# Twenty-six more filler matmuls on TensorE: twelve behind the first scores of the attention, fourteen ahead of the first gathered rows

## The chip, the cores and the metric

The kernel runs on one core of one Trainium2 chip. The metric is the time of one execution on the device in microseconds (us), the median of three runs. Smaller is better.

## What is computed

Three layers follow each other: an attention whose queries are pooled in pairs, a mixture of eight experts with one expert for each token, and a dense feed-forward layer.

```python
q_pool = q.reshape(B, H, S // 2, 2, D).mean(axis=3)        # B, H, S, D = 2, 8, 1152, 64
scores = np.matmul(q_pool, k.transpose(0, 1, 3, 2)) / np.sqrt(D)
attn = softmax(scores)                                     # max subtracted, sum + 1e-9
x = np.matmul(attn, v)                                     # brought to 1152 tokens x 512
...
do_compute = x @ w_skip > 0                                # the other tokens pass unchanged
e_idx = np.argmax(xc @ w_gate, axis=1)                     # one of 8 experts
y = gate_w * (np.maximum(xc @ w1[e], 0) @ w2[e])           # w1 512 x 1024, w2 1024 x 512
out[do_compute] = xc + y
...
h = x @ w_in                                               # 512 x 2048
return (h * np.tanh(softplus(h))) @ w_out                  # 2048 x 512
```

## The kernel before

**Order.** The program fixes the order of every engine's work by the order in which the Python code issues it. An engine takes its instructions one after the other, and a semaphore holds an instruction back until what it reads is there. TensorE is PE in the profile, VectorE is DVE, ScalarE is ACT, GpSimd is POOL, and SP is the queue that issues most DMAs.

**Attention** (lines 55 to 470). The work is cut into 72 tiles, nine for each of the eight heads. A tile is 128 pooled queries against all 1152 keys. The loop of line 405 runs once for each tile n, and in one round TensorE gets, in this order: the transposes of tile n-3 (`turn`, line 175, from the fourth round on), some matmuls with the values (`av_step`, line 216, once whole heads are ready), and the scores of tile n (`scores`, line 145). The scores of a tile fill the PSUM tile `s`, of which there is one; DVE scales them, writes them to SBUF as `scp` and takes their minimum (line 148, called the eviction below), and only then may the scores of the next tile be written. ACT then takes the exponential (line 159), and copies the transposed tile out of PSUM (line 198). Before the first scores, ten filler matmuls run (line 400); the loads of the first head arrive meanwhile.

**Filler matmuls.** `keep_warm` (line 473) issues n matmuls of a 128x128 tile of ones by a 128x512 tile of zeros, both bf16. Nobody reads what they write: in the attention the target is the tile `tp`, which the first transposes overwrite later, and in the routing a tile `warm`. `WARM` (line 43) holds the counts for the four places.

**Routing** (lines 478 to 621). Behind the last projection of the attention, DVE works out for each token its expert and its place in that expert's list. Matmuls on TensorE count and order the tokens (lines 511, 515, 537). Fillers stand before, between and behind these: 9 at line 509, 5 at line 532 and 15 at line 542. Then the first lists of tokens are known, and POOL issues two gathers of rows (line 625, `first(idx)`), which read the rows that the attention has just written to DRAM. TensorE next transposes the first gathered rows (line 1304, `turn(ps)`), does a column of the ordering (line 587), and then the first matmul of the first expert (line 637, `up`, tile `sa`), for which ACT copies the transposed rows (line 1305). Behind it stands the large part of the ordering (line 587 again). It gives the remaining lists: POOL then gathers the other rows, and behind its first further gather stand the memsets (line 830) for which SP waits with the loads of the experts' remaining weights (line 831).

**Experts and feed-forward layer** (lines 814 to 920, 1013 to 1215). The experts' matmuls lie in branches that are taken according to how many tokens an expert has. The feed-forward layer is a loop of 48 steps with matmuls of line 1101 and line 1155.

Of the kernel before, what the change touches and what calls it, by code (L numbers as in the profile page):

```python
# [39 lines left out]
BF16 = mybir.dt.bfloat16  # L40
KEEP = (0, 1, 4, 5, 2, 3, 6, 7)
PASS = ((0, 0), (0, 1), (1, 0))
WARM = (10, 9, 5, 15)
SPARE = (1.45, 1.45, 1.9, 1.45, 1.45, 0.75, 0.0, 1.75, 1.45)
OFF = (4, 7, 10, 13, 16, 19, 22, 25)
EARLY = (13, 16, 19, 45, 30, 39, 48, 57, 62, 65, 68)
# [8 lines left out]
def attention(tc, io, lg, rows, wdec, zero_out, late, xr, yg):  # L55
    nc = tc.nc
    with ExitStack() as ctx:
# [13 lines left out]
        tp = ps_t.tile([P, 2, 512], F32, name="tp")  # L71
# [3 lines left out]
        def load_wb(h):  # L75
            st["wb", h] = one.tile([P, XW], F32, name="wb", tag="wb", bufs=2)
            nc.sync.dma_start(st["wb", h], io["wb"][h])
# [5 lines left out]
        def load(h):  # L83
            for b, r in enumerate((xr, yg)):
                st["qr", h, b] = r.rearrange("p t f -> p (t f)")[:, :S].rearrange("p (a c) -> p a c", a=2)
                nc.sync.dma_start(st["qr", h, b], io["qt"][h, b])
            for b in range(B):
                st["k", h, b] = kq.tile([P, Q], F32, name=f"ks{b}", tag=f"ks{b}")
                nc.sync.dma_start(st["k", h, b], io["kt"][h, b])

        def load_v(h):
            vt = raw.tile([P, B, KC, D], F32, name="vt", tag="vt", bufs=2)
            nc.sync.dma_start(vt, io["vt"][h])
            st["v", h] = vt
# [15 lines left out]
        def first_head():  # L110
            near = (slice(0, Q // 2), slice(0, 320))
            far = tuple(slice(c.stop, Q) for c in near)
            ld = nc.sync.dma_start
            qr = []
            for b, r in enumerate((xr, yg)):
                qr.append(r.rearrange("p t f -> p (t f)")[:, :S].rearrange("p (a c) -> p a c", a=2))
                st["qr", 0, b] = qr[b]
                st["k", 0, b] = kq.tile([P, Q], F32, name=f"ks{b}", tag=f"ks{b}")
            ld(qr[0][:, :, near[0]], io["qt"][0, 0, :, :, near[0]])
            for c in (slice(0, HQ), slice(HQ, Q)):  # L120
                ld(st["k", 0, 0][:, c], io["kt"][0, 0, :, c])
            ld(qr[1][:, :, near[1]], io["qt"][0, 1, :, :, near[1]])
            ld(st["k", 0, 1], io["kt"][0, 1])
            for b in range(B):
                ld(qr[b][:, :, far[b]], io["qt"][0, b, :, :, far[b]])
            q_sum(0, 0, near[0], nc.vector)
            q_sum(0, 1, near[1], nc.gpsimd)
            for b in range(B):
                q_sum(0, b, far[b], nc.gpsimd)

        def scores(h, t):
            if t == 4:
                ops = [(slice(0, D), st["q", h, 0][:, 4 * P :], 0), (slice(D, P), st["q", h, 1][:, :D], 1)]
            else:
                b, c = t // 5, P * t if t < 4 else P * (t - 5) + D
                ops = [(slice(0, P), st["q", h, b][:, c : c + P], b)]
            scp = sc.tile([P, S], F32, name="scp", tag="scp")
            mx = sm.tile([P, 1], F32, name="mx", tag="mx")
            st["x", h, t] = scp, mx
            for j in range(2):  # L140
                cs = slice(HQ * j, HQ * j + HQ)
                for o, w, b in ops:
                    for half in range(2):
                        r = slice(D * half, D * half + D)
                        st["tick"] = nc.tensor.matmul(  # L145
                            s[o, half, j, :HQ], w[r], st["k", h, b][r, cs], start=True, stop=True
                        ).ins
            nc.vector.tensor_scalar(  # L148
                scp.rearrange("p (a c) -> p a c", a=4),
                s.rearrange("p a j c -> p (a j) c")[:, :, :HQ],  # L150
                -EXP_SCALE, -NEG, op0=ALU.mult, op1=ALU.min, accum_out=mx,
            )
# [16 lines left out]
        def turn(h, t, eight, nine, opened=None):  # L169
            e = st.pop(("e", h, t))  # L170
            for i in range(KC):
                for a in range(2):
                    q = slice(D * a, D * a + D)
                    to = eight[a][:, D * i : D * i + D] if i < 8 else nine[a]
                    nc.tensor.matmul(  # L175
                        to, e[q, P * i : P * i + P], io["ident"][q, q], start=i < 8 or a != opened, stop=True,
                        is_transpose=True, skip_group_check=True,
                    )
# [11 lines left out]
        def put_e(h, t, ks, v):  # L190
            b, tt = t // 5, t % 5
            if t == 4:
                for g in range(2):
                    to = etile(h, g)[:, ks, :, 256:].rearrange("p k b c -> p b k c")
                    nc.scalar.copy(to, v[:, :, :, 32 * g : 32 * g + 32])
            else:
                to = etile(h, tt // 2)[:, ks, b, P * (tt % 2) : P * (tt % 2) + P]
                nc.scalar.copy(to.rearrange("p k (a c) -> p a k c", a=2), v)  # L198
# [85 lines left out]
        def finish(h):  # L284
            norm(h)
            project(h, ovs, range(4), 1)
            xt = scale(h, ovs, 0)
            put(h, xt, 0, 9)
            dec_ops.insert(0, (0.28, lambda: logits(h, xt)))
# [109 lines left out]
        nseq = len(seq)  # L399
        keep_warm(nc, io, tp[:, 0], WARM[0])  # L400
        first_head()
# [3 lines left out]
        for n in range(nseq + 1):  # L405
            pos = n % 9
            h = n // 9
            m = n - 3
            run = n < nseq
            trn = 0 <= m < nseq  # L410
            if run:
                nxt = h + 1 < H
                if pos == 0 and nxt:
                    load(h + 1)
                if pos == 1:
                    load_wb(h)
                if pos == 4 and nxt:
                    sums = [0, 1]
                if pos == 7 and nxt:
                    load_v(h + 1)  # L420
            c = slice(512 - D, 512)
            if trn:
                opened = None
                if avq and avq[0][3] and not pend:
                    opened = avq[0][1]
                    c = slice(c.start - spot * D, c.stop - spot * D)
                    spot += 1
                else:
                    spot = 0
                turn(*seq[m], tph, [x[:, c] for x in ov], opened)  # L430
                put_e(*seq[m], slice(0, 8), tpk)
            if pend:
                finish(pend.pop(0))
            else:
                av_step((3 if len(avq) >= 9 else 2) if run else 6)
            if 0 < n <= nseq:
                expo(*seq[n - 1])
            if trn:
                put_e(*seq[m], slice(8, KC), ovs[:, :, c].unsqueeze(2))
            if pos == 3:  # L440
                ext_copy()
            if trn:
                if m % 9 == 4:
                    av_start(seq[m][0], 0)
                if m % 9 == 8:
                    av_start(seq[m][0], 1)
            if run:
                scores(*seq[n])
                if n == 6:
                    dec_load(0)  # L450
                    dec_load(1)
                if n in EARLY:
                    zero_out(EARLY.index(n))
            st["used"] = False
            if run and not fin:
                dec_run(SPARE[pos])
            if run and not st["used"]:
                if sums and pos + len(sums) > 7:
                    beside(q_sum(h + 1, sums.pop(0), slice(0, Q), nc.gpsimd))
                elif side:  # L460
                    beside(side.pop(0)())
                elif sums:
                    beside(q_sum(h + 1, sums.pop(0), slice(0, Q), nc.gpsimd))
            if fin:
                hf = fin.pop(0)
                pend = [hf]
# [6 lines left out]
def keep_warm(nc, io, out, n):  # L473
    for _ in range(n):
        nc.tensor.matmul(out, io["ones"], io["blank"], start=True, stop=True)


def routing(tc, io, lg, rt, tmp, ps, first, second, turn, kept):
# [29 lines left out]
    W = (T + 1) * E  # L508
    keep_warm(nc, io, warm, WARM[1])
    for s in range(1, T + 1):  # L510
# [20 lines left out]
    )  # L531
    keep_warm(nc, io, warm, WARM[2])
    tk4 = tk.rearrange("p t (c j) -> p t c j", j=4)
# [7 lines left out]

    keep_warm(nc, io, warm, WARM[3])

# [854 lines left out]
```

## Time and profile before

| | us |
|---|---|
| median of three runs | 577.96 |
| the three runs | 577.7, 577.96, 579.11 |
| the profiled execution, its own time | 581.02 |
| span of the profiled execution, first to last instruction | 579.1 |
| TensorE busy in that span | 544.2 (94%) |
| mean granted TensorE clock in that span | 0.975 of full speed |

The granted clock is told as a share of 2.4 GHz: 1.00 is 2.4 GHz and 0.50 is 1.2 GHz. In a row of the timeline the first number is the start in us from the start of the span, the second how long it lasted, and xN how many instructions the row merges; a bracket at its end tells how long the engine was idle before and what ended that.

### The profile page before, as it was taken

Reading aid. Unit: us, or ns where it says so; the run is one execution under the profiler, and the core shown is the slowest. Engines: PE = TensorE matmul, PEld = TensorE weight load, DVE = VectorE, ACT = ScalarE, POOL = GpSimd, SP = SyncE. Lnnn points to the kernel's source line nnn. Section 1 sums busy time; section 2 is a strip of 40 time slices with the busy share of each in tenths; the row PEclk is TensorE's granted clock in tenths of the full one; section 3 lists DMA queues with packets and bytes.
Section 4 is the critical chain, followed back from the end, with each engine's and each line's share of the span. In section 5 each row is a group of like instructions: output and inputs, shape, how many; then the busy total and the mean of one; then the engine's idle time right before and its main releaser. Section 6 shows DMA issues by size and latency. Waiting matters only on the chain. (4 is left out here: it accounts for less than half of the span.)

```text
span 579.1 us, 12048 instructions
## 1 busy us (share of the span) xinstructions
PE 544.2 (94%) x4781; PEld 402.4 (69%) x4781; DVE 372.0 (64%) x709; ACT 358.1 (62%) x663; POOL 95.9 (17%) x98
## 2 busy tenths in 40 slices
PE   6799999999999999789969989999999999999994
PEld 3566666766676667336724655898899998999982
DVE  3488888888988886610010026699986677666663
ACT  3888888888888885110112012799877766666562
POOL 1213454334533311240000110000000000000000
PEclk8899999999999999989978999999999999999998
DMA  7568867997978771279976095455112200010001
GB/s 251 205 207 285 281 231 276 318 340 238 311 262 301 224 260 58 76 217 400 401 278 257 24 343 199 130 190 174 55 37 87 77 0 2 0 57 2 0 1 59
DMA packets 50358, 103.03 MB, mean 178 GB/s; under 512 B 14043, under 2 KB 15451, under 8 KB 50288
## 3 DMA queue, kind: packets, MB, share of 16 engines
q1 hardware_dynamic: 47760, 95.99, 48.3%
q0 software_dynamic: 1296, 3.75, 2.1%
q10 hardware_dynamic: 1232, 2.36, 1.2%
q8 instruction: 43, 0.70, 0.5%
q14 instruction: 27, 0.22, 0.1%
HBM read 85.49 MB, written 17.04 MB: 177 GB/s over the span
## 5 line engine op out<-in xcount | busy, mean ns | idle before, releaser
L148 DVE TENSOR_SCALAR_CACHE_REDUCE scp<-s 128x1152 f32<-128x1152 f32 x72 | 97.7, 1357 | 35.9 <-PE s L145 24.9
L1101 PE MATMUL ph<-xT,wi 128*128 128x384 f32 x576 | 108.5, 337 | 0.0
L1101 PEld LDWEIGHTS ph<-xT,wi 128*128 128x128 f32 x576 | 102.2, 188 | 4.2
L145 PE MATMUL s<-ks,qs 64*128 64x288 f32 (+1 forms) x640 | 90.9, 432 | 7.1 <-DVE scp L148 5.5
L159 ACT ACTIVATE scp<-scp,mx 128x1152 f32<-128x1152 f32 x72 | 90.5, 1257 | 8.1 <-DVE scp L148 7.9
L1155 PE MATMUL po<-wo,gh 128*128 128x512 f32 x288 | 90.3, 394 | 0.8 <-ACT gh L1140 0.7
L198 ACT COPY eT<-tp 128x1024 f32<-128x1024 f32 x63 | 63.8, 1013 | 29.5 <-PE tp L175 29.0
L145 PEld LDWEIGHTS s<-ks,qs 64*128 64x128 f32 (+1 forms) x640 | 49.1, 177 | 42.9 <-DVE scp L148 17.5
L216 PE MATMUL ov<-eT,vt 128*64 128x288 f32 x540 | 78.3, 417 | 0.0
L1155 PEld LDWEIGHTS po<-wo,gh 128*128 128x128 f32 x288 | 52.9, 188 | 10.3 <-ACT gh L1140 1.5
L175 PEld LDWEIGHTS tp<-cst,scp 64*128 64x128 f32 x1145 | 48.0, 141 | 13.6 <-issue 4.4
L1155 PE MATMUL po<-wo,gl 128*128 128x512 f32 x144 | 57.2, 397 | 0.0
L1125 ACT ACTIVATE u<-u 128x384 f32<-128x384 f32 (+1 forms) x49 | 25.4, 519 | 46.6 <-DVE u L1119 46.1
L1145 DVE TENSOR_TENSOR gl<-s,gh 128x384 fp32r<-128x384 f32 (+1 forms) x49 | 27.0, 550 | 41.7 <-ACT gh L1140 41.5
L175 PE MATMUL tp<-cst,scp 64*128 64x64 f32 x1145 | 49.1, 225 | 0.0
L347 POOL TENSOR_TENSOR g<-wd 128x512 f32<-128x512 f32 x32 | 34.0, 1064 | 89.0 <-PE s L145 74.7
L216 PEld LDWEIGHTS ov<-eT,vt 128*64 128x64 f32 x540 | 33.6, 136 | 19.2
L1155 PEld LDWEIGHTS po<-wo,gl 128*128 128x128 f32 x144 | 27.0, 187 | 6.7 <-DVE gl L1145 1.0
L1127 ACT ACTIVATE r<-s,one 128x384 f32<-128x384 f32 (+1 forms) x49 | 30.0, 611 | 1.6
L1126 ACT ACTIVATE s<-u,one 128x384 f32<-128x384 f32 (+1 forms) x49 | 29.9, 611 | 1.6
L1119 DVE TENSOR_SCALAR u<-ph 128x384 f32<-128x384 f32 (+1 forms) x49 | 26.6, 545 | 6.5 <-PE ph L1101 6.4
L1134 DVE SCALAR_TENSOR_TENSOR r<-u,r 128x384 f32<-128x384 f32 (+1 forms) x49 | 26.9, 550 | 1.7
(195 smaller groups left out, 686.9 us busy)
## 6 DMA issues: line engine op xcount, KB each, us to landing
w<-w SPq DMA_DIRECT2D x32, 1024.0 KB, 9.5
wd<-wq SPq DMA_DIRECT2D x32, 512.0 KB, 6.0
wdec<-g SPq DMA_DIRECT2D x32, 256.0 KB, 5.5
vt<-vt SPq DMA_DIRECT2D x8, 576.0 KB, 7.3
ks<-kt SPq DMA_DIRECT2D x15, 288.0 KB, 6.2
ring<-wdec SPq DMA_DIRECT2D x16, 256.0 KB, 4.6
wr<-wdec SPq DMA_DIRECT2D x16, 256.0 KB, 2.7
xr<-qt SPq DMA_DIRECT2D x7, 576.0 KB, 5.9
```

What stands on the lines that cost most here:

```text
L145: st["tick"] = nc.tensor.matmul(s[o, half, j, :HQ], w[r], st["k", h, b][r, cs], start=True, stop=True).ins
L148: nc.vector.tensor_scalar(scp.rearrange("p (a c) -> p a c", a=4), s.rearrange("p a j c -> p (a j) c")[:, :, :HQ], -EXP_SCALE, -NEG, op0=AL ...
L159: nc.scalar.activation(scp, scp, AF.Exp, bias=mx, scale=-1.0, accum_out=st["sum", h][:, t : t + 1],)
L175: nc.tensor.matmul(to, e[q, P * i : P * i + P], io["ident"][q, q], start=i < 8 or a != opened, stop=True, is_transpose=True, skip_group_ch ...
L198: nc.scalar.copy(to.rearrange("p k (a c) -> p a k c", a=2), v)
L216: nc.tensor.matmul(acc[D * b : D * b + D, :288], st["v", h][:, b, kc], src[:, kc, b], start=(kc == 0), stop=(kc == KC - 1), skip_group_che ...
L347: side.append(lambda: tt(g, hf, hf, op=ALU.mult))
L1101: nc.tensor.matmul(ph, wi.w[i][:, a, P * k : P * k + P], xTs[c][b][:, k], start=(n == 0), stop=(n == 11),)
L1126: nc.scalar.activation(s[:, c], u[:, c], AF.Square, bias=one)
L1127: nc.scalar.activation(r[:, c], s[:, c], AF.Ln, bias=one)
L1145: nc.vector.tensor_tensor(gl[:, c], a["t"][1][:, c], gh[:, c].bitcast(F32), op=ALU.subtract)
L1155: nc.tensor.matmul(acc[j], g[a][:, P * j : P * j + P], wo[b][:, i], start=(i == 0 and n == 0), stop=(i == 15 and n == 2),)
```

## The change

Two things change. In the attention, six filler matmuls are issued behind the scores of the first tile and six behind those of the second (n of 0 and 1), into the same target `tp` as the ten at the start. In the routing, the count of fillers behind line 537, ahead of the transposes of the first gathered rows, goes from 15 to 29.

```diff
-WARM = (10, 9, 5, 15)
+WARM = (10, 9, 5, 29, 6)
...
             if run:
                 scores(*seq[n])
+                if n < 2:
+                    keep_warm(nc, io, tp[:, 0], WARM[4])
                 if n == 6:
                     dec_load(0)
```

## Rows read from the trace of the kernel before

**Rows 1.** Page, span in 40 slices: TensorE busy tenths, granted clock tenths.

```profile
PE   6799999999999999789969989999999999999994
PEclk8899999999999999989978999999999999999998
```

**Rows 2.** Windows: stretch, length, busy PE, PEld, DVE, ACT, POOL, clock, DMA, GB/s.

```profile
6.55:11.17 4.62, 1.64 (x13) 1.09 (x14) 2.73 (x4) 1.81 (x3) 2.38 (x3) 1.00 0.99 338
11.17:18.00 6.83, 5.79 (x52) 4.39 (x48) 2.73 (x4) 3.91 (x7) 0.00 (x0) 0.50 0.95 330
18.00:28.00 10.00, 7.06 (x106) 5.52 (x108) 4.14 (x8) 9.24 (x18) 2.89 (x3) 1.00 0.42 169
22.00:24.00 2.00, 1.07 (x22) 0.93 (x20) 1.37 (x2) 1.76 (x5) 1.40 (x1) 1.00 0.14 51
239.42:243.28 3.86, 0.33 (x4) 0.33 (x4) 1.38 (x9) 0.00 (x0) 1.64 (x2) 1.00 0.42 118
243.28:246.69 3.41, 2.90 (x35) 1.60 (x35) 2.24 (x8) 0.59 (x1) 0.95 (x1) 0.50 0.20 43
```

**Rows 3.** Timeline, TensorE, the scores of the first five tiles.

```profile
5.18 1.37 PE L145 MATMUL s<-ks,qs 64*128 64x288 f32 x8
...
8.02 1.24 PE L145 MATMUL s<-ks,qs 64*128 64x288 f32 x8 [1.47 <-DVE scp L148]
...
10.78 1.97 PE L145 MATMUL s<-ks,qs 64*128 64x288 f32 x8 [1.51 <-POOL qs L108]
...
14.21 2.29 PE L145 MATMUL s<-ks,qs 64*128 64x288 f32 x8 [0.50 <-DVE scp L148]
...
18.15 1.20 PE L145 MATMUL s<-ks,qs 64*64 64x288 f32 x16 [0.69 <-DVE scp L148]
```

**Rows 4.** Timeline, VectorE, the eviction of the third tile's scores.

```profile
12.78 1.36 DVE L148 TENSOR_SCALAR_CACHE_REDUCE scp<-s 128x1152 f32<-128x1152 f32 x1 [2.11 <-PE s L145]
```

**Rows 5.** Timeline, TensorE, routing, from the fifteen fillers on.

```profile
236.01 3.41 PE L475 MATMUL warm<-zero,ones 128*128 128x512 bf16 x15
...
242.96 0.88 PE L1304 MATMUL mt<-cst,yg 128*128 128x128 f32 x4 [3.53 <-DMA yg<-rows,idx]
...
244.56 2.94 PE L637 MATMUL sa<-w,xsT 128*32 128x256 f32 x32 [0.51 <-ACT xsT L1305]
...
247.44 0.47 PE L587 MATMUL ix<-r_B,r_A 128*128 128x72 f16 x9
...
248.43 0.63 PE L695 MATMUL mt<-cst,yg 128*128 128x128 f32 x4 [0.52 <-PE ix L587]
```

**Rows 6.** Timeline, TensorE, in the experts.

```profile
302.32 3.15 PE L637 MATMUL sa<-w,xsT 128*32 128x256 f32 x25 [2.52 <-issue]
304.88 3.68 PE L727 MATMUL sy<-w,hsT 128*32 128x256 f32 x32
...
334.02 1.93 PE L637 MATMUL sa<-w,xsT 128*32 128x256 f32 x32
...
336.75 1.93 PE L727 MATMUL sy<-w,hsT 128*32 128x256 f32 x32
```

**Rows 7.** Timeline, VectorE, GpSimd and SP in the routing.

```profile
244.52 0.95 POOL L625 DMA_INDIRECT xm<-rows,idx  x1 [3.16 <-DVE r_most L601]
...
245.57 0.83 DVE L584 TENSOR_TENSOR r_B<-r_B,cst 128x648 f16<-128x648 f16 x1
...
248.93 0.95 POOL L625 DMA_INDIRECT yt<-rows,idx  x1 [3.46 <-DVE spot L846]
...
249.99 13.09 SPq L831 DMA_DIRECT2D w<-w  x7
```

**Rows 8.** DMA issues: out<-in, queue, operation, count, us from issue to landing.

```profile
xm<-rows,idx POOLq DMA_INDIRECT x1, 3.5
```

**Rows 9.** Timeline, TensorE weight loads, one filler of the first ten.

```profile
2.43 0.15 PEld L475 LDWEIGHTS <-ones 128*128 128x128 bf16 x1 [0.28 <-issue]
```

**Rows 10.** Page, DMA queues: packets, MB, share of 16 engines.

```profile
q8 instruction: 43, 0.70, 0.5%
```

## The prediction

> **What bounds the kernel now.** I began with the page's forty slices: TensorE is busy all the time from the third slice to the end of the attention, and its granted clock is full there; the slices with gaps and with a lower clock are the first two, those around the routing and those of the experts [rows 1]. The change works in the first kind and the second, so the whole-kernel shares say little, and I went on to the granted clock by stretches. It tells two stories of the same form. From 6.55 to 11.17 us TensorE works 1.64 of 4.62 us, and at 11.17 its clock falls to 0.50, that is 1.2 GHz, and stays there to 18.00. From 239.42 to 243.28 it works 0.33 of 3.86 us, falls at 243.28, and is back at 246.69 [rows 2].
>
> The third view is the timeline of the front. Here TensorE and VectorE take turns on the single PSUM tile: scores 1.24 us, eviction 1.36 us, next scores. From the second tile's scores to the third's it is 10.78 - 8.02 = 2.76 us. At the low clock the scores take 1.97 (the fall lies inside them) and 2.29 us, and the two steps from 10.78 to 18.15 take 7.37 us in place of 2 x 2.76 = 5.52 [rows 3, 4]. So in the front TensorE's clock is on the path, since eviction and scores don't overlap. The fourth view is the routing: the first gathered rows arrive at 242.96, 3.53 us after the fillers ran out, and the transposes, ScalarE's copy and the first expert's matmul follow at the low clock [rows 5].
>
> **Part 1, six fillers behind the first two scores.** Added: 12 matmuls with their weight loads. Price of one: 15 fillers took 3.41 us in the routing [rows 5], 0.227 us each, so six take 1.36 us at full clock. The first gap is from 5.18 + 1.37 = 6.55 to 8.02, that is 1.47 us, the second from 8.02 + 1.24 = 9.26 to 10.78, 1.52 us [rows 3]. Both hold the six with 0.11 and 0.16 us to spare: cost nothing, covered by the evictions. If that cover went, each us of overrun would delay the next scores by a us. The fillers wait for nothing, and nobody waits for them: the eviction waits for the last score matmul ahead of them, and the target is first read after the transposes of the fourth round. No DMA and no other queue is passed.
>
> What they are to bring: TensorE then works 1.64 + 2 x 1.36 = 4.36 of the 4.62 us before the fall. That this keeps the clock up is not shown for this place; the nearest rows are the stretch behind 18.00, where it works 7.06 of 10.00 us, in bursts with gaps of like size, and the clock stays full [rows 2]. The value taken is that the fall at 11.17 goes. The gain: third scores 1.97 - 1.24 = 0.73, fourth 2.29 - 1.24 = 1.05, together 1.78; by the steps 7.37 - 5.52 = 1.85. I take **1.8 us**. Bounds: 1.85 if all goes, nothing if the clock falls all the same, and a loss under the slow rival below. What is late next is ScalarE, busy 9.24 of 10.00 us behind 18.00, still less than the turn of TensorE and VectorE, and the loads: the DMA engines are full up to 22 us, but at 22 to 24 their share is 0.14, all landed, and the values are wanted only in the tiles after that [rows 2]. From there on TensorE is busy without gaps to the end of the attention [rows 1], so a start 1.8 us earlier is an end 1.8 us earlier.
>
> **Part 2, 29 fillers for 15.** Added: 14 x 0.227 = 3.2 us on TensorE. They end at 236.01 + 3.41 + 3.2 = 242.6, and the gathered rows come at 242.96 [rows 5]: 0.34 us to spare, so they cost nothing. The gather is not moved by them, as it waits for writes to DRAM and for VectorE's list, which stands ahead of the fillers. Without that cover (rows landing half a us sooner) the overrun is at most those 0.5 us.
>
> The gap at 239.42 shrinks from 3.5 us to some 0.4, so the fall at 243.28 should go. The transposes then cost 0.63 instead of 0.88 (the row of 248.43 is the same four at full clock): 0.25. The first expert's 32 matmuls cost 1.93 instead of 2.94 (the row of 334.02 is the same at full clock): 1.01 [rows 5, 6]. Sum 1.26. What is late next: VectorE's mask for the large ordering ends at 245.57 + 0.83 = 246.40; it hangs on the tail ordering behind the transposes and moves up by about 0.2, to 246.2, while TensorE is free for it at 247.44 - 1.26 = 246.18. So the two meet, and the large ordering starts **1.2 us** earlier. With it go the transposes at 248.43, POOL's gather at 248.93 and the loads of the expert weights at 249.99 [rows 5, 7]. The other gather, of `xm`, lands at 244.52 + 3.5 = 248.0, moved up by 0.2 to 247.8 [rows 7, 8]; it is wanted behind the transposes that now start at 247.2 and last 0.63, so it just does not hold anything up. Bounds: 0 if the clock falls all the same, 1.26 if the mask does not hold, and 1.5, an estimate, if in another execution the low stretch also lies over the transposes at 248.43, the same four at another 0.25 us.
>
> **Sum.** 1.8 + 1.2 = 3.0 us. In the profiled execution's own time 581.02 - 3.0 = 578.0. That execution is 3.06 us above the median of the runs, 577.96; the saving is one of a few matmuls on the path and is carried over as it is: **575.0 us**.
>
> **Rivals.**
>
> *Only the routing's fall goes, because the front's fall is not there in a usual run.* The three runs lie between 577.7 and 579.11 and the profiled one at 581.02, so executions differ by about what the front is worth. For it: one trace can't say whether the fall at 11.17 is in every run, and the gaps ahead of it are short. Against: nothing in the front changes from run to run but arrival times. Time 577.96 - 1.2 = 576.8. The Trainium skill says in "TensorE: Matmul & The Clock Gate", Part 1, that the number of slow matmuls at a kernel's start differs from run to run, and gives 6, 11 and 14 for one kernel; by that rule this rival is what the median run would show, and no single trace here can show it.
>
> *The fillers don't hold the clock.* Zeros are streamed, no real data. Against it: the clock is full during the fifteen of the routing, and up to 3.9 us behind them [rows 2, 5]. Time 578.0, no change.
>
> *Slower, by the front.* If the clock is at 1.2 GHz when the six run, one takes 0.15 + 0.28 = 0.43 us, as at the start [rows 9], and six take 2.6 us against gaps of 1.47 and 1.52: the second and third scores start 1.1 us later each, and the second takes 0.75 longer. The point from which it decides is a pitch above 1.47 / 6 = 0.245 us. With the routing's gain kept: 577.96 + 2 x 1.1 + 0.75 - 1.2 = 579.7. Against it: the second scores take 1.24 us, so the clock was full by then [rows 3].
>
> *The code moves.* TensorE's program grows by 26 matmuls and 26 weight loads, and code arrives in pieces, 43 packets of together 0.70 MB [rows 10]. In the experts TensorE stands still for 2.52 us in the middle of a row of 32 like matmuls, for nothing that the profile shows, and works at the low clock afterwards: 3.15 us for 25 where 32 take 1.93, and 3.68 for 1.93 [rows 6]. If that is an edge between pieces, it moves by those 52 instructions. If it goes, 2.52 and up to (3.15 - 1.51) + (3.68 - 1.93) = 3.4 us are gained: 569.1 to 572.5. If a like stall comes at another branch: 577.5 to 580.9.
>
> **How the numbers follow.** Both falls go, 574.0 to 576.2: 0.56, the forecast. Only the routing's: 0.20. No fall goes: 0.06. Slower by the front: 0.05. Code moves to the good: 0.07; to the bad: 0.06. The range is 572.5 to 578.0; it leaves out the last part of the good code case, the bad one and the slow front, less than 2 in 10. A measurement of this kernel can tell about 0.3%, 1.7 us, from no change: faster is below 576.2, slower above 579.7. Faster: 0.56 + 0.07 less a little, 0.62. Same: 0.20 + 0.06 and the near edges of the code and front cases, 0.30. Slower: 0.08.
>
> **What would show it.** Right: third and fourth scores of 1.24 us with a granted clock of 1.00 from 5 to 240 us; fifth scores near 16.35; the gathered rows' transposes 0.63 and the first `sa` row 1.93 us, the loads of line 831 some 3.0 us earlier than 249.99. Wrong: second scores later than 8.02 (fillers too long), a fall at another place in the front, transposes that start behind the 29th filler, a gain that shows at 250 us and is gone at 340 (taken back among the branches).

## The result, and the profile after

The changed kernel took 571.73 us (median of four runs, 571.64 to 571.77) where the kernel before took 578.21 beside it (four runs, 577.7 to 579.11). The ratio is 0.9886, with a 95% interval from 0.9869 to 0.9903: 6.5 us faster. The forecast was 575.0 with a range down to 572.5, so the direction was right and the gain more than double. The profiled execution of after took 571.73 us, with a span of 569.9; that of before took 581.02, more than any other run of that kernel in this study (the others lie between 574.8 and 580.5). A second trace of the kernel before, e5 below, stands beside it for that reason.

Two lines are added above the routing, so line 637 of before is 639 of after; experiments add a few more. The page of after, the 40 slices that answer to [rows 1], TensorE's busy tenths and its granted clock:

```profile
PE   8799999999999999989989989999999999999994
PEclk9999999999999999999989999999999999999998
```

The clock's 8 in slices 1, 2 and 18 of before is gone, and in the experts 7 and 8 in slices 21 and 22 have become one 8. The table says what each stage is worth. A mark is the first matmul of a stage on TensorE in the trace, and a figure is the time from one mark to the next, in us.

| from, to | before | before again (e5) | after |
|---|---|---|---|
| start, first scores | 5.18 | 5.51 | 5.97 |
| first scores, sixth scores | 15.73 | 13.97 | 14.18 |
| sixth scores, last projection | 209.6 | 209.6 | 209.6 |
| projection, transposes of the first gathered rows | 12.42 | 12.34 | 11.75 |
| those transposes, first `sa` row | 1.61 | 1.84 | 1.33 |
| first `sa` row, `sa` of `xgT` | 5.24 | 5.75 | 5.23 |
| `sa` of `xgT`, `sy` of line 727 | 6.65 | 5.67 | 5.31 |
| that `sy`, `la` (line 768) | 5.28 | 3.58 | 3.58 |
| first `ht` of `hs`, second | 6.64 | 7.78 | 5.80 |
| second `ht`, third | 35.53 | 35.35 | 30.85 |
| fourth `ht`, fifth | 5.23 | 4.79 | 6.35 |

What is left out is equal to within 0.3 us in all three. Against the profiled execution of before, the last matmul of after comes 9.4 us sooner: 1.55 from the front, of which 0.8 is given back by a later start, 4.0 around the routing, 4.4 in the experts, 0.3 behind them. Against e5 it comes 6.4 us sooner: 0.7 lost in the front, start included, 2.0 gained around the routing and 4.9 in the experts, 0.2 behind them. So the largest part of both comparisons is the experts, where the change adds and removes nothing.

TensorE's timeline of after in the front, the scores of the first five tiles and the two groups of six fillers, answering to [rows 3]:

```profile
5.97 1.60 PE L145 MATMUL s<-ks,qs 64*128 64x288 f32 x8
7.50 1.47 PE L477 MATMUL tp<-zero,ones 128*128 128x512 bf16 x6
9.04 1.24 PE L145 MATMUL s<-ks,qs 64*128 64x288 f32 x8
10.21 1.47 PE L477 MATMUL tp<-zero,ones 128*128 128x512 bf16 x6
11.80 1.24 PE L145 MATMUL s<-ks,qs 64*128 64x288 f32 x8
14.49 1.24 PE L145 MATMUL s<-ks,qs 64*128 64x288 f32 x8 [0.91 <-DVE scp L148]
17.39 1.20 PE L145 MATMUL s<-ks,qs 64*64 64x288 f32 x16 [1.08 <-DVE scp L148]
```

Third and fourth scores take 1.24 us: the fall of [rows 3] is gone. From the first to the fifth scores it is 11.42 us, where before had 12.97. The fifth scores still come at 17.39 and not near 16.35, as the first start 0.8 us later and take 1.60 us.

The routing of after on TensorE, answering to [rows 5], and VectorE's mask, answering to [rows 7]:

```profile
235.49 6.21 PE L477 MATMUL warm<-zero,ones 128*128 128x512 bf16 x28 [0.16 <-issue]
241.53 0.60 PE L1306 MATMUL mt<-cst,yg 128*128 128x128 f32 x4
...
242.86 1.93 PE L639 MATMUL sa<-w,xsT 128*32 128x256 f32 x32 [0.53 <-ACT xsT L1307]
244.74 0.47 PE L589 MATMUL ix<-r_B,r_A 128*128 128x72 f16 x9
246.71 0.63 PE L697 MATMUL mt<-cst,yg 128*128 128x128 f32 x4 [1.50 <-DVE spot L848]
```

```profile
243.85 0.83 DVE L586 TENSOR_TENSOR r_B<-r_B,cst 128x648 f16<-128x648 f16 x1
```

Two things are to be seen. The transposes at 241.53 have no idle time ahead of them: they stand behind the last filler and no longer wait for the rows. And the large ordering, at 244.74, came 2.70 us sooner than in [rows 5], but the transposes behind it only 1.72 us, with 1.50 us of idle time ahead of them. In both kernels they start 2.03 us behind the end of VectorE's mask (243.85 + 0.83 = 244.68 and 246.71; 245.57 + 0.83 = 246.40 and 248.43 in [rows 5, 7]).

The experts of after on TensorE, answering to [rows 6], and the granted clock (the column ahead of the last two) of the stretch around the first rows:

```profile
292.54 0.41 PE L708 MATMUL ht<-cst,hs 128*128 128x128 f32 x2 [1.82 <-issue]
292.88 3.13 PE L639 MATMUL sa<-w,xsT 128*32 128x256 f32 x32
295.76 2.46 PE L729 MATMUL sy<-w,hsT 128*32 128x256 f32 x32
...
328.95 1.93 PE L639 MATMUL sa<-w,xsT 128*32 128x256 f32 x31
332.90 0.40 PE L639 MATMUL sa<-w,xsT 128*32 128x256 f32 x1 [2.02 <-issue]
```

```profile
292.00:300.00 8.00, 7.00 (x76) 3.56 (x78) 1.30 (x4) 1.19 (x4) 0.00 (x0) 0.79 0.97 345
```

The row of `sa` that was cut after seven matmuls by 2.52 us in [rows 6] is whole. A stand of 2.02 us has come at another place, after 31 of 32 at 328.95, where before had a whole row and stood for 1.09 us a little later.

### The profile page after: what moved, and what is told of

Read it like the earlier page. It is cut to its first block, busy times and chain, and to the rows that moved or that the text cites. A ratio compares the mean times of both kernels' runs of the same rounds, so it can differ in the third digit from the quotient of the medians.

```text
span 569.9 us, 12098 instructions
## 1 busy us (share of the span) xinstructions
PE 542.8 (95%) x4805; PEld 402.3 (71%) x4807; DVE 372.0 (65%) x709; ACT 358.1 (63%) x663; POOL 95.9 (17%) x98
## 3 DMA queue, kind: packets, MB, share of 16 engines
q10 hardware_dynamic: 1232, 2.36, 1.2%
## 5 line engine op out<-in xcount | busy, mean ns | idle before, releaser
L145 PE MATMUL s<-ks,qs 64*128 64x288 f32 (+1 forms) x640 | 89.4, 427 | 5.2 <-DVE scp L148 4.9
```

What stands on the lines that cost most here:

```text
L145: st["tick"] = nc.tensor.matmul(s[o, half, j, :HQ], w[r], st["k", h, b][r, cs], start=True, stop=True).ins
```

## The experiments

In the expectations of e1 to e8, theory A says that the gain is the clock in the two places where fillers were added; theory B says that it is also the place of TensorE's code. The expectations of e13 to e16 use the same letters for two theories of their own, which they state. The kernels e1 to e4, e5 to e8, e9 to e12 and e13 to e16 each ran on one chip, beside the kernel before (578.56, 578.52, 578.34 and 578.70 us). "Four-column" matmuls are fillers that stream four columns in place of 512: 26 of them took 0.79 us, and they and their weight loads are 52 instructions like those of 26 fillers.

**e1, the front alone.** As the change, but 15 stays 15 (24 instructions more).

```diff
-WARM = (10, 9, 5, 15)
+WARM = (10, 9, 5, 15, 6)
+                if n < 2:
+                    keep_warm(nc, io, tp[:, 0], WARM[4])
```

> Only the six fillers behind the first two scores; the routing keeps its 15. Theory A (granted clock alone, as in the prediction): the fall in the front goes, 1.8 us faster than before, about 576.4, and the stretch behind the routing looks as before, with its fall near 242.5 and the stand of 2.5 us in the middle of 32 like matmuls near 300. Theory B (the program's place in its code pieces matters too): TensorE's program is longer by 24 instructions from here on, so that stand moves ahead of the branch's target or goes, and the gain is 1.8 plus 3 to 5 us, 571 to 573.5.

573.66 us (571.64 to 573.87), ratio 0.9903 [0.9874, 0.9932].

**e2, the routing alone.** 29 for 15, no fillers in the front (28 instructions more).

```diff
-WARM = (10, 9, 5, 15)
+WARM = (10, 9, 5, 29)
```

> Only the 29 fillers for 15 ahead of the first gathered rows; none behind the first scores. Theory A: 1.2 us faster than before, about 577.0, the fall in the front stays, the one behind the gather goes. Theory B: 28 instructions more ahead of the experts, so also 3 to 5 us from the experts' stand, 572 to 574.

572.36 us (571.69 to 572.85), ratio 0.9895 [0.9871, 0.9918]. Each half gives some five or six us, so the halves don't add up to the whole. In neither trace is the cut row of [rows 6] there. In the routing of e2 the 29 fit as the prediction said, with 0.36 us to spare:

```profile
234.40 6.43 PE L475 MATMUL warm<-zero,ones 128*128 128x512 bf16 x29
241.19 0.66 PE L1304 MATMUL mt<-cst,yg 128*128 128x128 f32 x4 [0.36 <-DMA yg<-rows,idx]
```

**e3, the code alone.** The kernel before with 26 four-column matmuls behind the fifteen fillers: 52 instructions more, as in the change, but only 0.79 us of TensorE's time, all of it inside the wait for the rows.

```diff
     keep_warm(nc, io, warm, WARM[3])
+    for _ in range(26):
+        nc.tensor.matmul(warm[:, :4], io["ones"], io["blank"][:, :4], start=True, stop=True)
```

> The kernel before with 26 matmuls of only four columns behind its 15 fillers, in the time in which TensorE waits for the gathered rows (26 x 0.07 = 1.8 us of the 3.5 us). TensorE's program is as much longer behind the routing as in the changed kernel, 52 instructions, but the clock is not helped. Theory A: no change, 578.2 within 0.5, both falls stay. Theory B: the stand of 2.5 us near 302 goes and what follows runs at the higher clock sooner, 3 to 6 us faster, 572 to 575.

572.46 us (571.26 to 573.34), ratio 0.9899 [0.9872, 0.9925]: 6.1 us, nearly all that the change brings. Its experts on TensorE:

```profile
293.66 0.41 PE L708 MATMUL ht<-cst,hs 128*128 128x128 f32 x2 [1.81 <-issue]
294.00 1.93 PE L639 MATMUL sa<-w,xsT 128*32 128x256 f32 x32
295.75 1.91 PE L729 MATMUL sy<-w,hsT 128*32 128x256 f32 x32
```

No cut, and no low clock. From the second to the third `ht` it is 29.17 us, 6.2 to 6.4 less than in both traces of before.

**e4, the clock alone.** Fillers in fp32 give as long a work in fewer instructions: one long and one short filler in each gap of the front, two and one for nine, one and one for five, seven and one for fifteen. The count of instructions is that of before.

```diff
+def keep_long(nc, io, out, n):
+    for _ in range(n):
+        nc.tensor.matmul(out, io["void"][:, :P], io["void"], start=True, stop=True)
...
-    keep_warm(nc, io, warm, WARM[3])
+    keep_long(nc, io, warm, 7)
+    keep_warm(nc, io, warm, 1)
```

> The fillers of the changed kernel by time, but in the number of instructions of the kernel before: fp32 fillers, each of which makes two weight loads and two matmuls of 0.43 us in place of one of 0.22. Front: 1.08 us behind each of the first two scores; routing: 1.95, 1.08 and 6.28 us as with 9, 5 and 29. Behind the routing TensorE's program is where it was before. Theory A: as the changed kernel, 571.7 within 1. Theory B: both falls go, and that is all, 1.5 to 3 us faster, 575.2 to 576.7, with the stand near 302 still there.

575.41 us (573.75 to 578.82, ten runs), ratio 0.9948 [0.9928, 0.9967]: 3.15 us. The cut is back, and longer:

```profile
295.57 0.63 PE L648 MATMUL sa<-w,xsT 128*32 128x256 f32 x7
299.17 3.14 PE L648 MATMUL sa<-w,xsT 128*32 128x256 f32 x25 [2.97 <-issue]
```

The gain equals the forecast's sum, and yet it can't be added to that of e3: 3.15 + 6.1 would be 9.2, and the change brings 6.5. The profiled execution of e4 is one of its slower ones (576.53), so its trace can't place all of the 3.15. It does show that part of it lies at and behind the cut, where e4 adds nothing: from the second to the third `ht` it takes 34.29 us, where before and e5 take 35.53 and 35.35.

**e5, the kernel before once more.**

> The kernel before, unchanged, for a second trace of it: the one on which the prediction rests is of an execution of 581.02 us, above all 13 others of that kernel (577.2 to 579.7). Expected by both theories: 577 to 580 us, the stand of 2.5 us in the middle of 32 like matmuls near 300 there again. Open: whether the wait of 1.8 us ahead of the matmul at 256.45 was of that execution alone; in four other kernels it was 0.46 to 0.55.

578.01 us (eight runs, 576.61 to 579.83), ratio 0.9987 [0.9968, 1.0006]. Its trace has the cut of 2.52 us as before has it. But the front has no fall: third and fourth scores take 1.24 us with no filler behind the first two.

```profile
8.37 1.24 PE L145 MATMUL s<-ks,qs 64*128 64x288 f32 x8 [1.47 <-DVE scp L148]
11.13 1.24 PE L145 MATMUL s<-ks,qs 64*128 64x288 f32 x8 [1.52 <-POOL qs L108]
...
13.83 1.24 PE L145 MATMUL s<-ks,qs 64*128 64x288 f32 x8 [0.90 <-DVE scp L148]
```

**e6, code moved by 256 instructions.** 128 four-column matmuls: 22 behind each of the first two scores, 84 behind the fifteen.

```diff
+def keep_short(nc, io, out, n):
+    for _ in range(n):
+        nc.tensor.matmul(out[:, :4], io["ones"], io["blank"][:, :4], start=True, stop=True)
...
+                if n < 2:
+                    keep_short(nc, io, tp[:, 0], 22)
...
     keep_warm(nc, io, warm, WARM[3])
+    keep_short(nc, io, warm, 84)
```

> The kernel before with 128 matmuls of four columns, 256 instructions with their weight loads: 22 behind each of the first two scores (0.5 us of gaps of 1.5 us) and 84 behind the 15 fillers (2.1 us of a wait of 2.1 to 3.5 us). If what matters is where the branch's target lies in a piece of code of 256 instructions (in straight code a fetch of 16 KB comes about every 256 instructions), the stand comes back in the same place, after 7 of the 32 matmuls, and the time goes back to 578.5 within 1. If any longer program helps (the routing's gap being filled, say), it is near 572.

576.41 us (ten runs, 573.03 to 577.82), ratio 0.9962 [0.9942, 0.9982]. The cut is back, after exactly seven of 32:

```profile
295.04 1.08 PE L645 MATMUL sa<-w,xsT 128*32 128x256 f32 x7
298.56 3.15 PE L645 MATMUL sa<-w,xsT 128*32 128x256 f32 x25 [2.45 <-issue]
```

So its place repeats with 256 instructions: it is there at 0 (before, e4, e5) and at 256, and absent at 24, 28, 52, 140 and 150. TensorE's queue of code (queue 8, [rows 10]) moves 16,384 bytes at a time, and in straight code (the feed-forward loop of before, 433 to 559 us) I count 251 to 260 instructions from one such packet to the next. The time itself was missed by 2 us; part of that is the coming of the rows, which e13 explains.

**e7 and e12, code moved by 140 and 150.** The change with 20 fillers, and 53 or 58 four-column matmuls behind them, meant to put the second stand out of the way too.

```diff
-WARM = (10, 9, 5, 15)
+WARM = (10, 9, 5, 20, 6)
...
     keep_warm(nc, io, warm, WARM[3])
+    keep_short(nc, io, warm, 53)
```

> The changed kernel with 20 fillers for 29 and 53 matmuls of four columns behind them: 140 instructions more than before in place of 52. By the place in the code: the stand of 2.0 us that the changed kernel has within 32 matmuls near 331 (66 instructions behind a branch's target) would move ahead of that target and go, and the wait at the branch near 291 stays about 1.8; 569.5 to 570.5. By theory A: as the changed kernel, 571.7 within 0.5.

> The changed kernel with 20 fillers and 58 four-column matmuls: 150 instructions more than before. With 140, the edge that had stood TensorE still near 331 lay 24 instructions ahead of a branch's target, and that branch took 4.4 us in place of 0.36; with 52, an edge 32 instructions ahead of the other branch's target was harmless. With 150 the edge lies 34 ahead of this target: the branch is expected to be short again and no stand to be left in either place, 569.5 to 571. If any edge near a target hurts, 573 to 575.

573.49 us (571.02 to 576.69), 0.9904 [0.9873, 0.9936], and 571.41 (570.52 to 572.48), 0.9888 [0.9872, 0.9904]. Both are no better than the change. The stand of 2.02 us at 332.90 went, but ahead of the next branch's target came one of 3 us; of e12:

```profile
328.83 0.41 PE L714 MATMUL ht<-cst,hs 128*128 128x128 f32 x2 [3.00 <-PEq L805]
```

The branch ahead of it took 4.29 us in e12 and 4.36 in e7, and 0.35 to 0.36 in all other kernels. Of e12, the four branches of that line on TensorE (shortest, median and longest in ns):

```profile
L805 PEldq COMPARE_BRANCH  x4: 70/238/4292, 245.9 to 324.4; - x4
```

My rule for where a piece of code may end without harm was wrong; none that fits all kernels was found.

**e8, 25 fillers.** The change with 25 fillers and four four-column matmuls, 52 instructions in all.

```diff
-WARM = (10, 9, 5, 15)
+WARM = (10, 9, 5, 25, 6)
...
     keep_warm(nc, io, warm, WARM[3])
+    keep_short(nc, io, warm, 4)
```

> The changed kernel with 25 fillers for 29 and four of four columns behind them, so that TensorE's program is as long: the fillers end 0.8 us sooner. In the trace of the changed kernel the transposes of the gathered rows start straight behind the 29th filler, without a wait, so the fillers may hold them up by up to 0.8 us. If they do, 571.0 to 571.6; if the rows come later than that as a rule, 571.7 within 0.3.

573.85 us (572.08 to 574.7), ratio 0.9923 [0.9899, 0.9946]: not better than 29, and above both figures expected. In its trace the rows' transposes start 2.57 us behind GpSimd's second gather instead of 3.33 in after, so the hold by the fillers was there and went; but TensorE then stood 2.30 us ahead of line 727, which is taken up at the end.

**e9, e10 and e11, one chip.** The change again; the kernel of e3 again; and the change with 15 fillers and 14 four-column matmuls behind them, which is the front's fillers with the code of the change. The edit of e11:

```diff
-WARM = (10, 9, 5, 15)
+WARM = (10, 9, 5, 15, 6)
...
+                if n < 2:
+                    keep_warm(nc, io, tp[:, 0], WARM[4])
...
     keep_warm(nc, io, warm, WARM[3])
+    keep_short(nc, io, warm, 14)
```

> The changed kernel once more, in one job with the next two, to see what the clock is worth where the code lies in the good place. 571.7 to 572.5 by every theory.

> The kernel before with 26 four-column matmuls, so the code of the changed kernel without its fillers. If the clock is worth 3 us wherever the code lies, 3 us above the changed kernel, about 575; if the traces are right that it is worth about 0.6 in the front (13.8 to 14.2 us against 13.8 to 15.7 from the first scores to the sixth) and 0.2 to 0.9 in the routing, 0.8 to 1.5 us above it.

> The changed kernel's six and six in the front, 15 fillers in the routing as before, and 14 four-column matmuls behind them, so that the code lies as in the changed kernel. Against the changed kernel it tells what the 14 more fillers of the routing are worth by the clock: 0.2 to 0.9 us by the traces, 1.2 by the prediction. Against the run with the code alone, what the front is worth.

e9: 571.66 us (571.14 to 572.3), 0.9888 [0.9873, 0.9903]. e10: 571.08 (570.44 to 572.08), 0.9877 [0.9861, 0.9893]. e11: 569.0 (568.49 to 571.06), 0.9844 [0.9828, 0.9859]. On this chip the code is worth 7.3 us, the front's fillers another 2.1, and the 14 further fillers cost 2.7. In e9 the clock falls all the same, later: at 247.13, in a row that takes 3.65 us in after, e3 and e11.

```profile
247.13 5.22 PE L639 MATMUL sa<-w,xgT 128*64 128x512 f32 x16 [0.35 <-ACT xgT L750]
```

**e13 to e16, what the front's fillers bring.** In the six traces so far where the code ahead of the first list stands, by count, where it stood (before, e2 to e5, e10), GpSimd's first gather starts 2.63 to 2.75 us behind its list of tokens; in the eight others it is 1.24 to 1.27. So the 2.1 us of e11 could be code once more. e13 has 12 four-column matmuls in the middle of the attention and none in the front, e14 the fp32 fillers of e4 in the front with the code in place; both have 52 instructions more in the end. e15 is e3, e16 is e11. The edits of e13 and of e14:

```diff
+                if n == 60:
+                    keep_short(nc, io, tp[:, 0], 12)
...
     keep_warm(nc, io, warm, WARM[3])
+    keep_short(nc, io, warm, 14)
```

```diff
+                if n < 2:
+                    keep_long(nc, io, tp[:, 0], 1)
+                    keep_warm(nc, io, tp[:, 0], 1)
...
-    keep_warm(nc, io, warm, WARM[1])
+    keep_long(nc, io, warm, 2)
+    keep_warm(nc, io, warm, 1)
...
-    keep_warm(nc, io, warm, WARM[2])
+    keep_long(nc, io, warm, 1)
+    keep_warm(nc, io, warm, 1)
...
     keep_warm(nc, io, warm, WARM[3])
+    for _ in range(26):
+        nc.tensor.matmul(warm[:, :4], io["ones"], io["blank"][:, :4], start=True, stop=True)
```

> The kernel before with 12 four-column matmuls behind the scores of tile 60 (24 instructions, in the middle of the attention, none in the front) and 14 behind the fifteen fillers: the instruction counts of e11_front_code from tile 60 on, without its fillers in the front. Theory A (a 16 KB piece of TensorE's code is fetched while the rows are written to DRAM, in every trace without 24 more instructions ahead of the routing, and holds up the last packets of that write and so POOL's first gather by 1.4 us): the gather starts 1.25 us behind the list of tokens, not 2.65, and the time is that of e10_code_again less 1.4, 569.3 to 570.3 us if that is 571.1. Theory B (what e11 gained over e10 was the clock in the front): the gather stays at 2.65 us behind its list or its coming sooner is worth nothing, and the time is that of e10, 571.1 us.

> The kernel before with fp32 fillers in the two gaps of the front, fewer instructions in the fillers at lines 509 and 532 by as much, and 26 four-column matmuls behind the fifteen fillers: the clock is kept in the front, and the code ahead of the first gather stands where it stood. Theory A: the gather starts 2.65 us behind its list, and the time is that of e10_code_again less what the front's fall costs in the mean, some 0.7 us (it was there in two traces of five without fillers, at 1.8): 570.4 us if e10 is 571.1. Theory B: the time is that of e11_front_code, 569.0 us.

> The kernel of e10_code_again on the same chip as the two new ones. Both theories: 571.1 us (570.4 to 572.1), the gather 2.65 us behind its list.

> The kernel of e11_front_code on the same chip. Both theories: 569.0 us (568.5 to 571.1), the gather 1.25 us behind its list. Theory A: equal to e13_mid_code less at most 0.7; theory B: 2.1 less than e13 and equal to e14.

| | median, us | runs | ratio | list to gather, us |
|---|---|---|---|---|
| e15, code | 572.46 | 572.0 to 573.9 | 0.9905 [0.9876, 0.9934] | 2.63 |
| e13, code moved in the attention too | 572.32 | 570.83 to 574.26 | 0.9906 [0.9875, 0.9937] | 1.25 |
| e14, code and the front's clock | 571.90 | 571.41 to 572.61 | 0.9892 [0.9863, 0.9920] | 2.63 |
| e16, fillers in the front and code | 571.30 | 570.62 to 573.57 | 0.9891 [0.9860, 0.9922] | 1.26 |

The last column is as theory A said, in 18 of 18 traces. The list and the first gather in e15, then in e13 (two views each, VectorE and GpSimd):

```profile
235.27 0.16 DVE L547 TENSOR_SCALAR idx<-ix 128x2 int32<-128x2 f32 x1 [0.56 <-PE ix L537]
237.90 1.18 POOL L627 DMA_INDIRECT yg<-rows,idx  x1 [7.99 <-DVE r_li L572]
```

```profile
235.00 0.16 DVE L553 TENSOR_SCALAR idx<-ix 128x2 int32<-128x2 f32 x1 [0.56 <-PE ix L544]
236.25 1.20 POOL L633 DMA_INDIRECT yg<-rows,idx  x1 [6.62 <-DVE r_tl L569]
```

And the DMA view of seven us around them, e15 first: packets of the code's queue, and the two writes of rows with the us from issue to landing.

```profile
q8 instruction: 1, 0.02, 0.9%
...
rows<-xt SPq DMA_DIRECT2D x1, 160.0 KB, 2.4
rows<-xt SPq DMA_DIRECT2D x1, 128.0 KB, 3.4
```

```profile
rows<-xt SPq DMA_DIRECT2D x1, 160.0 KB, 2.2
rows<-xt SPq DMA_DIRECT2D x1, 128.0 KB, 2.1
```

In e15 a packet of code, 16 KB and some 1 us, lies among the packets of the write that the gather waits for, and the write's last packets come 1.3 us later. In e13 the code came some 3.5 us sooner, and the view has no row of its queue. In all 18 traces the gather starts 0.90 us behind the landing of the later write.

The times were not as theory A said: e13 takes as long as e15 at the median, and their ranges overlap over most of their length. The profiled executions differ as expected (570.83 and 572.21). e16 is 2.3 us above e11, the same kernel on another chip, so differences of a us or two between such variants can't be settled by five or six runs. Put together, the code alone has 572.15 (e3, e10 and e15, 14 runs), code with the front's fillers 570.76 (e11 and e16, 11 runs), and the change 571.73 (8 runs).

## Why the prediction was wrong, point by point

**The step that failed is the sum: it has no term for the place of the code.** The sum is 3.0 us of clock; the 52 instructions stand in it at nothing and appear only as a rival, "The code moves", at 0.07. That rival had its mechanism right: the stand of [rows 6] is an edge between pieces of code, and 52 instructions move it. Where 52 instructions that do next to nothing were added, the kernel took 572.46, 571.08 and 572.46 us on three chips, 6.1 to 7.3 us below before, while the clock brought 0.4 beside such code. The chance of 0.07 was the mistake. Together with the bad sign it was 0.13, as if such a move were an accident; but a change that adds instructions ahead of such an edge moves it, as all five counts between 24 and 150 did here. What was open was only whether the new places hurt, and the trace had the old place as one of the worst of its rows: 2.52 us, with the low clock behind it.

The rival's price was too low as well. Its 569.1 to 572.5 us count the 3.0 us of clock too, so the code alone was put at 2.5 to 5.9 us. That the kernel's 571.73 lies between them is luck in part: too much for the clock and too little for the code.

The Trainium skill says in "Runtime: NRT & Kernel Launch", section "Instruction fetch mechanics", that code comes in blocks of 16 KiB, 256 instructions, that crossing into the next is mostly hidden, and that a taken branch to a target outside the blocks at hand must wait for its fetch. The traces agree on the size and on the waits at branches: the branch ahead of the cut row took 2.2 to 4.1 us in before, e1, e2, e4, e5 and e6 and 0.4 to 0.5 in e3, e7 to e16 and the change. The four branches of its line on TensorE, in before and then in after (shortest, median and longest in ns):

```profile
L797 PEldq COMPARE_BRANCH  x4: 70/220/2357, 248.4 to 337.2; - x4
```

```profile
L799 PEldq COMPARE_BRANCH  x4: 70/222/477, 246.7 to 326.9; - x4
```

They differ on what is hidden: the cut of 2.5 us lies inside straight code, a little behind a branch, and a packet of code among the writes of rows cost the gather 1.4 us. That a taken branch lies behind each of these stands is not shown by every trace.

**The front: mechanism likely right, size wrong for the median.** The fall is gone in all ten traces with fillers of the change's length there. The term, 1.8 us, was read from one execution and carried to the median "as it is". Of seven traces with no filler in the front two have the fall (15.73 and 15.04 us from first to sixth scores) and five have not (13.8 to 14.0): in the mean it costs (1.8 + 1.1) / 7 = 0.4 us. None of ten against two of seven can still be chance. e14 against e15 gave 0.6, less than the runs of e15 differ among themselves. Here the rival "only the routing's fall goes" was right about the front (about the routing it was not), and so was the rule of the Trainium skill that it cited, that the number of slow matmuls at the start differs from run to run: the same ten fillers at the start took 3.63 us in before, 3.96 in e5 and 4.42 in after. What the front's fillers also do, and the prediction did not see, is to move the code by 24 instructions out of the writes of rows.

**The routing: 1.2 us became nothing, and the 29 are not free.** From the transposes of the first rows to those behind the large ordering, the stretch that was to lose 1.2, it is 5.18 us in after, 5.47 in before and 5.94 in e5: 0.3 to 0.8. Three links of the step failed. First, "29 cost nothing" was true with the rows coming as in before (e2, 0.36 us to spare against 0.34 forecast). But the rows came sooner in after: behind GpSimd's second gather they take 2.59 us in e1 (238.35 to 240.94), and in after that gather stood at 238.19, so the rows were there at 240.8, and the fillers held the transposes until 241.53, some 0.75 us. Two parts that were each costed against the trace of before met each other. Second, the large ordering, 2.70 us sooner, brought the transposes behind it only as much as VectorE's mask came sooner: 1.72 us, and 1.50 of idle time was left. The prediction looked at the mask as the start of the ordering; it did not see what else stands between the mask and the transposes. In the trace's records that is four register loads of line 686 on TensorE, from 246.50 to 248.22 in before and from 244.78 to 246.50 in after, 0.41 to 0.60 us from one start to the next. They stand behind the large ordering in TensorE's order, and in all 18 traces the first starts 0.1 us behind the end of the mask. In before (shortest, median and longest in ns):

```profile
L686 PEldq TENSOR_LOAD <-cnt x8: 296/306/491, 246.5 to 297.8; - x8
```

Third, the fall was moved about as often as removed: of the seven traces without it at the gather (after, e2, e4, e7, e8, e9, e12), four have one later, before 260 us (so have before and e16, behind the one at the gather). From the `sa` of `xgT` to `la`, behind the place, the seven have a mean of 10.4 us (8.9 to 12.4), and the eleven with it 9.5 (8.9 to 11.9). On one chip 29 cost 2.7 us against 15 with the same code; over all runs it is 1.0 (571.73 against 570.76). That they cost something is likely, how much is not settled.

**The sum.** Clock in both places was to bring 3.0 us. Beside code that stands at the same place it brings 0.4 (572.15 to 571.73), less than these runs can tell from nothing. With the code in its old place it did bring 3.15 (e4). Why the two don't add up stays open. One part shows in e4's trace: the low clock around the cut lasts 6.83 us there, 10.24 in before, e5 and e6, and the third `ht` comes 1.1 to 1.2 us sooner behind the second. What is saved there is gone with the cut anyway, so it can't count twice. One trace doesn't show that this holds at the median, nor where the rest lies.

**The other rivals.** "Slower by the front" didn't come: the six take 1.47 us, and the second scores stand 3.07 us behind the first instead of 2.84, because the first took 1.60: its first two matmuls took 0.85 us each, its last four 0.40. "The fillers don't hold the clock" found no support in the front: ten traces with them, and no fall. Two signs that were to prove the forecast wrong were named there and came: transposes straight behind the 29th filler, and second scores later than 8.02 (9.04, of which 0.8 is the later start and 0.2 the long first scores, not fillers that are too long). Of the signs of being right, the clock (no fall before 293 us), the scores, the first transposes (0.60 us) and the first `sa` row (1.93) came too, so those signs could not tell a gain of 3 us from one of 0.4.

**Still open.** Which distance between the end of a piece of code and a branch's target hurts: at the first place 32 instructions ahead were harmless, at the second 24 and 34 were not. And what delays line 727: in before, e7, e8 and e16 TensorE is idle for 1.6 to 2.3 us ahead of it, and each time the clock is low behind it (5.28 us to `la` instead of 3.58). One step further back is on record: line 727 starts 0.4 us behind the start of ScalarE's copy to `hT` (line 712) in these four and in after, and in these four that copy starts 1.2 to 1.9 us behind the matmuls that it reads, with ScalarE idle for 0.8 to 1.5. In before those matmuls ended at 254.66:

```profile
256.03 0.37 ACT L712 COPY hT<-ht 128x256 f32<-128x256 f32 x1 [1.30 <-PE ht L706]
```

What holds ScalarE no trace shows.

## What to carry to other kernels

When an edit changes the number of instructions ahead of branches, run it beside a kernel with as many instructions that do next to nothing: here that control alone brought 6.1 to 7.3 us, as much as the change. A stand in the middle of a row of like matmuls, with nothing that it waits for, is worth moving for its own sake, and e7 and e12 show that it can then come back ahead of another branch. A saving read from one profiled execution should be looked up in a second one before it is carried to the median, and parts that are each harmless against the old trace must be costed against each other's effect.

## What was not expected of the hardware

- A packet of TensorE's code (16 KB) among the last packets of a DRAM write delayed that write from 2.1 to 3.4 us, and the engine that waited for it is GpSimd.
- The place of a stand repeats with 256 instructions to the matmul: seven of 32 in before, e4, e5 and e6.
- Branches of one line on TensorE took 0.35 to 0.5 us or 2.2 to 4.4 at two places of the program, by the place of the code. Full DMA engines are not needed for it: their share was 0.30 during the branch of 2.36 us in before (294.0 to 296.4 us), 1.02 during that of 4.29 in e12 (324.4 to 328.7), and 1.01 during the stand of 2.52 in before (299.8 to 302.3).
- Four register loads on TensorE put 1.7 us between a mask on VectorE and the next matmuls. Four more stand in the 1.82 us ahead of the `ht` at 292.54 in after (290.96 to 292.48).
- A four-column filler takes 0.03 us where one of 512 columns takes 0.23, so instructions can be added almost without time.
